# Value weights loaded as whole rows into both row halves, with a new order of the opening, in a linear attention and MLP kernel

## The chip, the cores and the metric

The kernel runs on one core of a Trainium2 chip. The metric is the device time of one execution in microseconds. The core has five engines with instruction queues of their own: TensorE (PE; its weight loads are shown as PEld), VectorE (DVE), ScalarE (ACT), GpSimd (POOL) and SyncE (SP), which here only issues DMAs. Each queue runs in order: an instruction that waits holds up all those behind it on its engine.

## What is computed

The input x has 2048 rows of 576 values in bfloat16. A pre-norm mixer with 32 heads of 18 dimensions is followed by a pre-norm MLP with 4608 hidden values:

```python
qkv = (x @ wqkv).reshape(B, S, 3, H, Dh)            # x: layer norm of the input
pq = jnp.einsum("bhsd,hdf->bhsf", q, w_phi)
pk = jnp.einsum("bhsd,hdf->bhsf", k, w_phi)
phi_q = concatenate([softmax(pq), softmax(-pq)])    # 36 features per head
phi_k = concatenate([softmax(pk), softmax(-pk)])
kv = jnp.einsum("bhsf,bhsd->bhfd", phi_k, v)
z = jnp.einsum("bhsf->bhf", phi_k)
num = jnp.einsum("bhqf,bhfd->bhqd", phi_q, kv)
den = jnp.einsum("bhqf,bhf->bhq", phi_q, z)[..., None] + 1e-6
h = x_in + (num / den) @ wo
out = h + gelu(layernorm(layernorm(h)) @ w1 + b1) @ w2 + b2
```

## The kernel before

The 2048 rows are 16 tiles of 128, taken in pairs p = 0 to 7; x stays in on-chip memory as `xh`. The contraction over 576 input features is done in nine chunks of 64 (`KC`, `KH`). One tile of a pair uses partitions 0 to 63 of TensorE and the other 64 to 127, side by side, so the weights `wkp` (keys), `wv` (values), `wqp` (queries) and `wo` have to stand in both halves of the partitions: rows `c * 64 + k` of the matrix at partition k, and again at 64 + k. This is `project` (L420): 9 chunks x 2 halves = 18 matmuls of 288 columns for one pair and half of the heads (`i` = 0 or 1).

The order of the whole kernel is written out by hand from L771 on, one call after the other, and the queues follow it. The opening does the following.

- **Loads.** `load_wk` (key weights), `load_x`, `load_values` (L163) and `load_wq` (L597, query weights, five DMAs in rows of 252 bytes) are all issued on SP. The value weights come in two DMAs, columns 0 to 287 and 288 to 575, each as 64 partitions x 9 chunks x 288 columns (rows of 576 bytes), to partitions 0 to 63 only.
- **Copies.** `copy_values` (L171) copies them on GpSimd into partitions 64 to 127, in four parts (column half i; chunks 0 to 4 or 5 to 8).
- **Key folds.** The key weights are turned (`flip_mm`, `flip_ev`) and multiplied per head with w_phi on TensorE: `fold_k_mm` (L376, ten matmuls for one chunk), and `fold_k_ev` (L388) moves the product from PSUM to `wkp`. The folds come in the order of chunks 0, 4, 8, 3, 7, 1, 2, 6, 5, and all nine are evacuated by ScalarE (the group L389).
- **Normalisation.** `stats` (L287, VectorE, two tiles per pair), `power` (L298, GpSimd, the inverse deviation), `centre` (L305, GpSimd) and `scale` (L308, ScalarE or VectorE) write the normalised pair to one of three buffers `lnb`. The pair is then turned, features onto partitions: pairs 0 and 1 on TensorE (`turn_x_mm`, `turn_x_ev`), the later ones by a DMA transpose on SP (`turn_dma`, L320).
- **Projections.** `key_mm` and `value_mm` project, `key_exp` (L458) writes exp(+) and exp(-) on ScalarE, `key_sum` (VectorE) and `key_weigh` (GpSimd) make the softmax of them, `value_ev` moves the values to `vals`, whose last column per head is 1 (`ones`, L224, GpSimd), and `sums` (L554) adds this tile's part to `acc_kv` in PSUM.

All the PSUM tiles of this stage but `acc_kv` come from the pool `two`, which has three buffers of two banks, taken in turn: a fold, a turned half pair or a projection can only start when the tile three before it has been evacuated. Per opening that is: folds 3 to 5, the two parts of `turn_x_mm(1)`, `key_mm(0, 0)`, `key_mm(0, 1)`, `value_mm(0, 0)` and so on.

SP's queue in the opening is, in order: key weights (three DMAs), x tiles 2 to 3 and 4 to 7, values (two), x tiles 8 to 11, query weights (five), `turn_dma(2)`, `load_wo(2)`, `turn_wq(4)`, `load_wo(0)`, `turn_wq(1)`, `turn_dma(3)`, the other `turn_wq`, `turn_dma(4)`, x tiles 12 to 15, `load_wo(3)`. A DMA on SP also waits until an earlier one, whose completion semaphore it takes over, has landed; there are eight of these for plain DMAs and transposes from SP and ScalarE together, used in turn.

Later on, `query_mm` and `query_exp` make the query features, `turn_q` transposes them on SP's queue, `combine_mm` multiplies them with the tables, and `divide` (L654, VectorE) divides by the denominators and writes `ob`, which is turned to `oT` and multiplied with `wo` (`residual_mm`, L692). The order of the features in `ob` has to be that of the rows of `wo`: before, place k = e * 32 + h of chunk c holds feature h * 18 + 2c + e, and `load_wo` (L606) fetches it in four DMAs (row half, e), each to 32 partitions in rows of 1152 bytes. From about 85 us on the MLP runs (`up`, `down`), with the other blocks' attention in between.

Of the kernel before, what the change touches and what calls it, by code (L numbers as in the profile page):

```python
# [8 lines left out]
P = 128  # L9
# [6 lines left out]
D = 576  # L16
NH = 32
DH = 18
# [7 lines left out]
HALF = D // 2  # L26
HH = NH // 2
VW = DH + 1
KC = 9
KH = 64  # L30
# [13 lines left out]
def kernel(  # L44
# [13 lines left out]
    nc = tc.nc  # L58
# [33 lines left out]
    wo = persist.tile([P, KC, D], BF16, name="wo", tag="wo")  # L92
# [10 lines left out]
    ob = [persist.tile([P, KC, 2, KH], BF16, name=f"ob{i}", tag=f"ob{i}") for i in range(2)]  # L103
# [56 lines left out]
            A_wqkv[0:512, D + f0 : D + f1].rearrange("(c p) f -> p c f", p=P),  # L160
        )

    def load_values(i):  # L163
        nc.sync.dma_start(
            wv[0:KH, :, i * HALF : (i + 1) * HALF],
            A_wqkv[:, 2 * D + i * HALF : 2 * D + (i + 1) * HALF].rearrange(
                "(c k) f -> k c f", k=KH
            ),
        )

    def copy_values(i, part, copy):  # L171
        cs = slice(i * HALF, (i + 1) * HALF)
        ks = slice(part * 5, 5 + part * 4)
        copy(wv[KH:P, ks, cs], wv[0:KH, ks, cs])  # L174

    wphi_rows = A_w_phi.rearrange("h d f -> (h d) f")

# [44 lines left out]
        )  # L222

    def ones():  # L224
        nc.gpsimd.memset(vals[:, :, :, DH], 1.0)

    def window_masks():
        full = small.tile([P, KW * WH], FP32, name="full", tag="full")
# [129 lines left out]
    def folded_whole(name, c, m):  # L358
        return flight[name, c].rearrange("p b f -> p (b f)")[:m, SPAN : SPAN + D]
# [13 lines left out]
    def turn_wq(c):  # L373
        nc.sync.dma_start_transpose(wT[:, :, c * P : (c + 1) * P], wq[:, c, :])

    def fold_k_mm(c):  # L376
        flight["k", c] = two.tile([P, 2, 512], FP32, name="pW", tag="two")[:, :, :]
        for g in range(NG):
            k = P if g < NG - 1 else 72
            for a in range(2):  # L380
                nc.tensor.matmul(
                    folded_part(g, "k", c, slice(a * KH, (a + 1) * KH)),
                    wT[:k, g, c * KH : (c + 1) * KH],
                    bd[:k, g, 0 : GH[g], :].rearrange("p h f -> p (h f)"),
                    start=True, stop=True,
                )

    def fold_k_ev(c, copy):  # L388
        copy(wkp[:, c, :], folded_whole("k", c, P))  # L389

    def fold_mm(name, c):
# [62 lines left out]
    phik, phiq, phiT = {}, {}, {}  # L454

    def key_mm(p, i):
        features("k", wkp, p, i, PLAIN)
# [139 lines left out]
    def load_wq():  # L597
        for c in range(NC):
            m = P if c < NC - 1 else 64
            src = A_wqkv[c * P : c * P + m, 0 : NG * 126]  # L600
            nc.sync.dma_start(
                wq[:m, c, :].rearrange("p (g f) -> p g f", g=NG)[:, :, 0:126],
                src.rearrange("p (g f) -> p g f", g=NG),
            )

    def load_wo(part):  # L606
        half, e = divmod(part, 2)
        r0 = half * KH + e * 32
        nc.sync.dma_start(
            wo[r0 : r0 + 32, :, :], A_wo.rearrange("(h c e) f -> e h c f", c=KC, e=2)[e]  # L610
        )

    def load_biases():
# [39 lines left out]
            leave_home(("phiT", p, a))  # L653

    def divide(t):
        o = ob[t // 2 % 2][:, :, t % 2, :].rearrange("p c (e h) -> p c e h", e=2)
        rec = small.tile([P, NH], FP32, name="rec", tag="rec")
        for w0, w1_ in BANKS:
            h0, h1 = FIRST[w0], min(NH, w1_ * WH)
            pv = products[t][w0 // 6][:, 0 : (h1 - h0) * VW].rearrange("p (h v) -> p h v", v=VW)  # L660
            nc.vector.reciprocal(rec[:, h0:h1], pv[:, :, DH])  # L661
            nc.vector.tensor_tensor(  # L662
                o[:, :, :, h0:h1],
                pv[:, :, 0:DH].rearrange("p h (c e) -> p c e h", e=2),
                rec[:, h0:h1].rearrange("p (u v h) -> p u v h", u=1, v=1).to_broadcast(
                    [P, KC, 2, h1 - h0]
                ),
                ALU.mult,
            )
# [107 lines left out]
    window_masks()  # L777
    load_x(2, 4)
    load_x(4, 8)
    load_values(0)  # L780
    load_values(1)
    stats(0, 1)
    power(0)
    centre(0, 0)
    scale(0, 0, act)
# [35 lines left out]
    fold_k_mm(7)  # L821
    fold_k_ev(7, act)
    fold_k_mm(1)
    fold_k_ev(1, act)
    fold_k_mm(2)
# [25 lines left out]
    load_wo(2)  # L851
    power(3)
    key_exp(0, 0)
    key_sum(0, 0)
    key_exp(0, 1)
    value_ev(0, 0, act)
    copy_values(1, 0, gps)
    turn_wq(4)
    load_wo(0)
    key_mm(1, 0)  # L860
# [70 lines left out]
    key_weigh(3, 1, 1, pool)  # L931
    fold_mm("q", 2)
    fold_ev("q", 2, act)
    load_wo(3)
    stats(6, 0)
    key_sum(3, 0)
    key_weigh(3, 1, 0, pool)
# [372 lines left out]
```

## Time and profile before

| what | us |
|---|---|
| median of 3 runs | 392.02 (391.94 to 392.32) |
| the profiled execution | 392.69 |
| its span | 391.0 |
| TensorE busy | 383.6 |
| VectorE, ScalarE, GpSimd busy | 163.5, 163.7, 128.2 |
| MLP matmuls, up (L1150) and down (L1194) | 141.3 and 143.3 |
| the four copies of the value weights (L174) | 5.0 |
| nine key fold evacuations on ScalarE (L389) | 5.06 |

The span runs from the first to the last instruction that the profiler saw; the execution's own time is 1.7 us longer. Times of single instructions count from the start of the span. Successive instructions of VectorE and ScalarE overlap by some 0.08 to 0.1 us in the records, so a row's duration is a little more than the pace at which such instructions follow each other. An entry of a timeline ends with the idle time before it and, after the arrow, what ended it.

### The profile page before, as it was taken

To read this page: it belongs to the slowest core of one execution; us is meant where nothing else is said; L and a number is where in the kernel's file an instruction comes from. 1 tells how busy PE (TensorE), PEld (TensorE's weight loads), DVE (VectorE), ACT (ScalarE), POOL (GpSimd) and SP (SyncE) were. 2 spreads that over 40 slices of the span, in tenths; PEclk is the share of its full clock that TensorE was granted. 3 is DMA by queue.
4 is the path that set the end of the run, shared out by engine and by line. 5 is a ranking of instruction groups with operands and counts; after the bars stand their busy time and mean duration, and the time that the engine had idled before them with its cause. 6 is when DMAs were issued, how large, how long until landed. Compare 5 with 4: busy or idle time off the path is not lost.

```text
span 391.0 us, 10251 instructions
## 1 busy us (share of the span) xinstructions
PE 383.6 (98%) x4492; PEld 267.2 (68%) x4493; DVE 163.5 (42%) x367; ACT 163.7 (42%) x290; POOL 128.2 (33%) x167
## 2 busy tenths in 40 slices
PE   8899999999999999999999999999999999999997
PEld 4687777779878887844457887444677764447773
DVE  6989894595249388590029322000480000000100
ACT  3978887678501850056650000666300026661000
POOL 8899999214604564144003111000031110000120
PEclk9999999999999999999999999999999999999999
DMA  8999749999655666643005542000041000000000
GB/s 220 189 182 175 163 98 184 227 300 254 206 106 104 95 107 134 107 61 62 0 2 63 90 106 48 16 1 2 2 102 50 17 17 0 2 2 0 17 29 18
DMA packets 76108, 34.76 MB, mean 89 GB/s; under 512 B 63026, under 2 KB 73536, under 8 KB 76064
## 3 DMA queue, kind: packets, MB, share of 16 engines
q1 hardware_dynamic: 75376, 32.47, 41.9%
q0 software_dynamic: 400, 1.35, 1.3%
q8 instruction: 35, 0.57, 0.6%
q10 hardware_dynamic: 288, 0.30, 0.3%
q14 instruction: 9, 0.07, 0.1%
HBM read 16.53 MB, written 2.36 MB: 48 GB/s over the span
## 4 chain that ended last, share of the span: by engine, by line
PE 94%; DVE 4%; POOL 1%; issue 1%; POOLq 0%
PE po L1194 36%; PE ph L1150 36%; PE pk L426 7%; PE pa L697 5%; PE pv L426 4%; PE acc_kv L562 2%; PE pw L250 1%; PE pn L648 1%; DVE st L293 1%; POOL wv L174 1%; DVE ob L662 0%; PE pW L396 0%; DVE shared L260 0%; PE pT L338 0%; DVE shared L314 0%
## 5 line engine op out<-in xcount | busy, mean ns | idle before, releaser
L1172 ACT ACTIVATE home<-ph,b1col 128x512 bf16<-128x512 f32 (+1 forms) x180 | 98.5, 598 | 169.6 <-PE ph L1150 166.3
L1194 PE MATMUL po<-w,home 128*128 128x288 bf16 (+2 forms) x1151 | 143.3, 286 | 0.1
L1150 PE MATMUL ph<-shared,w 64*128 64x512 bf16 (+2 forms) x1638 | 141.3, 332 | 0.1
L1194 PEld LDWEIGHTS <-home 128*128 128x128 bf16 x1152 | 109.2, 98 | 32.3 <-issue 1.8
L1150 PEld LDWEIGHTS <-w 64*128 64x128 bf16 x1638 | 80.3, 94 | 60.0 <-issue 1.0
L1198 DVE TENSOR_TENSOR ot<-po,hb 128x288 bf16<-128x288 f32 (+2 forms) x32 | 14.5, 454 | 106.5 <-PE po L1194 100.7
L1183 POOL TENSOR_TENSOR hb<-xh,b2bc 128x576 f32<-128x576 bf16 x16 | 20.4, 1272 | 104.6 <-DVE ot L1198 95.2
L426 PEld LDWEIGHTS <-home 64*128 64x128 bf16 x864 | 42.0, 94 | 10.8 <-issue 1.1
L512 POOL TENSOR_TENSOR padded<-home,rq 128x540 bf16<-128x540 bf16 x32 | 34.8, 1101 | 36.4 <-DVE rq L504 14.9
L256 POOL TENSOR_TENSOR rs<-va,mhalf 128x1 f32<-128x1 f32 x16 | 8.8, 550 | 105.0 <-DVE va L254 105.0
L706 DVE TENSOR_TENSOR xh<-pa,xh 128x288 bf16<-128x288 f32 x32 | 13.2, 449 | 71.6 <-PE pa L697 71.6
L483 POOL TENSOR_TENSOR phik<-phik,rk 128x576 bf16<-128x576 bf16 x32 | 36.4, 1164 | 1.4 <-PE pv L426 0.9
L477 DVE TENSOR_REDUCE sk<-phik 128x64 f32<-128x1152 bf16 x16 | 21.2, 1327 | 5.4 <-ACT phik L448 5.4
L448 ACT ACTIVATE home<-pk 128x576 bf16<-128x576 f32 x32 | 18.9, 649 | 6.9 <-PE pk L426 5.7
L503 DVE TENSOR_REDUCE sk<-home 128x64 f32<-128x1152 bf16 x16 | 21.0, 1313 | 0.0
L426 PE MATMUL pv<-wv,home 64*128 64x288 bf16 x288 | 20.9, 283 | 0.1
L426 PE MATMUL pk<-wqp,home 64*128 64x288 bf16 x288 | 20.0, 283 | 0.2 <-ACT home L448 0.2
L448 ACT ACTIVATE phik<-pk 128x576 bf16<-128x576 f32 x32 | 18.7, 652 | 3.1 <-PE pk L426 3.1
L426 PE MATMUL pk<-shared,home 64*128 64x288 bf16 x288 | 19.9, 283 | 0.0
L661 DVE RECIPROCAL rec<-pn 128x18 f32<-128x18 f32 (+1 forms) x32 | 8.0, 250 | 27.9 <-PE pn L648 27.9
L697 PE MATMUL pa<-wo,shared 64*128 64x288 bf16 x288 | 18.8, 283 | 0.0
L697 PEld LDWEIGHTS <-shared 64*128 64x128 bf16 x288 | 13.9, 94 | 4.3 <-issue 0.5
(78 smaller groups left out, 209.0 us busy)
## 6 DMA issues: line engine op xcount, KB each, us to landing
w<-in_B_w_dram SPq DMA_DIRECT2D x21, 432.0 KB, 7.0
out_dram<-ot SPq DMA_DIRECT2D x15, 144.0 KB, 1.9
xh<-in_A_x_dram SPq DMA_DIRECT2D x3, 576.0 KB, 7.3
wo<-in_A_wo_dram SPq DMA_DIRECT2D x4, 324.0 KB, 6.3
w<-in_B_w_dram POOLq DMA_DIRECT2D x3, 432.0 KB, 10.5
wv<-in_A_wqkv_dram SPq DMA_DIRECT2D x2, 324.0 KB, 9.9
w<-in_A_wqkv_dram SPq DMA_DIRECT2D x4, 157.5 KB, 8.7
wqp<-wqp SPq DMA_DIRECT2D x2, 288.0 KB, 3.9
```

Source lines behind the costliest of these rows:

```text
L426: nc.tensor.matmul(dst[:, a, 0:HALF], lhs[rows, c, :], w[rows, slot, i * HALF : (i + 1) * HALF], start=(n == 0), stop=(n == KC - 1),)
L448: nc.scalar.activation(rows[:, :, i * HH : (i + 1) * HH, s, :], flight[key, p, i][:, :, 0:HALF].rearrange("p a (h f) -> p a h f", f=DH), A ...
L477: nc.vector.tensor_reduce(sk[:, :, :], part_of(dst, i), AX.X, ALU.add)
L483: eng.tensor_tensor(part, part, flight["r" + key, p, i][:, a, :].rearrange("p (h o) -> p h o", o=1).to_broadcast([P, NH, DH]), ALU.mult,)
L503: nc.vector.tensor_reduce(sk[:, :, :], part_of(phiq[p], i), AX.X, ALU.add)
L512: eng.tensor_tensor(padded[:, a, g0 * P : (g0 + 5) * P].rearrange("p (g k) -> p g k", k=P)[:, :, 0:STEP].rearrange("p g (h f) -> p g h f", ...
L697: nc.tensor.matmul(pa[a], oT[p % 2][rows, c, :], wo[rows, c, cs], start=(c == 0), stop=(c == KC - 1),)
L1150: nc.tensor.matmul(ph[half][:, lo:hi], w1[p_ // 9][rows, c, p_ % 9 * P : (p_ % 9 + 1) * P], ln2T[rows, c, base + lo : base + hi], start=(c ...
L1172: nc.scalar.activation(hidden(m), ph[half][:, 0:width], AF.Gelu_apprx_tanh, bias=b1col[:, m : m + 1], scale=1.0,)
L1183: nc.gpsimd.tensor_tensor(hb[:, :], xh[:, t, :], b2bc[:, :], ALU.add)
L1194: nc.tensor.matmul(po[:, :], hidden(m)[:, i_ * P : (i_ + 1) * P], w2[m // 18][:, m % 18, cs], start=(j == 0), stop=(j == NM - 1),)
L1198: nc.vector.tensor_tensor(ot[:, cs], po[:, :], hb[:, cs], ALU.add)
```

## The change

The value weights come by DMA into both halves of the partitions, as whole rows of 576 columns (1152 bytes): `load_values(e, half, eng)` brings chunks 0 to 4 (e = 0) or 5 to 8 (e = 1) to the lower or the upper 64 partitions. There are four such DMAs, on SP's queue at the place of the two. The copies on GpSimd are gone.

```diff
-    def load_values(i):
-        nc.sync.dma_start(
-            wv[0:KH, :, i * HALF : (i + 1) * HALF],
...
-    def copy_values(i, part, copy):
-        cs = slice(i * HALF, (i + 1) * HALF)
-        ks = slice(part * 5, 5 + part * 4)
-        copy(wv[KH:P, ks, cs], wv[0:KH, ks, cs])
+    def load_values(e, half, eng):
+        c0, c1 = ((0, 5), (5, KC))[e]
+        eng.dma_start(
+            wv[half * KH : (half + 1) * KH, c0:c1, :],
+            A_wqkv[c0 * KH : c1 * KH, 2 * D : 3 * D].rearrange("(c k) f -> k c f", k=KH),
+        )
```

The opening is put in another order. `ones` goes to VectorE, ahead of the key flips. The fold of chunk 7 is evacuated by VectorE, both scalings of pair 1 follow right behind it on VectorE, and `stats(2, 1)`, `power(2)` and `stats(3, ...)` come later. `scale(2, 0)` moves to VectorE, and `scale(2, 1)` behind `key_exp(0, 0)` on ScalarE. `key_mm(0, 0)` takes the chunks in the order in which they were folded (`fold_order`).

```diff
     stats(2, 0)
-    ones()
     fold_k_mm(8)
     fold_k_ev(8, act)
     power(1)
-    stats(2, 1)
-    scale(1, 0, vec)
     fold_k_mm(3)
     fold_k_ev(3, act)
-    copy_values(0, 1, gps)
     fold_k_mm(7)
-    fold_k_ev(7, act)
+    fold_k_ev(7, dve)
+    scale(1, 0, vec)
+    scale(1, 1, vec)
...
     load_wq()
+    fold_k_ev(6, act)
+    turn_x_mm(1)
+    fold_k_ev(5, act)
+    stats(2, 1)
     power(2)
-    centre(2, 0)
-    stats(3, 0)
-    fold_k_ev(6, act)
-    scale(1, 1, vec)
-    stats(3, 1)
-    turn_x_mm(1)
     centre(2, 1)
-    copy_values(1, 1, gps)
-    copy_values(0, 0, gps)
     turn_x_ev(1, 0, dve)
-    fold_k_ev(5, act)
+    turn_x_ev(1, 1, dve)
     key_mm(0, 0)
     key_mm(0, 1)
+    key_exp(0, 0)
+    scale(2, 0, vec)
     scale(2, 1, act)
-    scale(2, 0, act)
     turn_dma(2)
-    turn_x_ev(1, 1, dve)
+    stats(3, 0)
+    stats(3, 1)
     stats(4, 0)
     stats(4, 1)
     value_mm(0, 0)
-    load_wo(2)
     power(3)
-    key_exp(0, 0)
```

`wo` comes in two DMAs, one for each half of the partitions, at the places of `load_wo(0)` and `load_wo(1)`; partition k holds rows 9k to 9k + 8 in one run. `divide` writes the features in the order that belongs to it: place k = 2h + e of chunk c holds feature h * 18 + 9e + c.

```diff
+    def load_wo(half):
         nc.sync.dma_start(
-            wo[r0 : r0 + 32, :, :], A_wo.rearrange("(h c e) f -> e h c f", c=KC, e=2)[e]
+            wo[half * KH : (half + 1) * KH, :, :],
+            A_wo.rearrange("(k c) f -> k c f", c=KC),
         )
...
             nc.vector.tensor_tensor(
-                o[:, :, :, h0:h1],
-                pv[:, :, 0:DH].rearrange("p h (c e) -> p c e h", e=2),
+                o[:, :, h0:h1, :],
+                pv[:, :, 0:DH].rearrange("p h (e c) -> p c h e", e=2),
```

The number of matmuls is the same, and no line from `key_mm(1, 0)` on moves, but for the places of the two pieces of `wo` that fall away.

More of the change, by code (lines that the diff above doesn't have):

```diff
@@ L224, in ones @@
     def ones():
-        nc.gpsimd.memset(vals[:, :, :, DH], 1.0)
+        nc.vector.memset(vals[:, :, :, DH], 1.0)
     def window_masks():
@@ L374, in turn_wq @@
         nc.sync.dma_start_transpose(wT[:, :, c * P : (c + 1) * P], wq[:, c, :])
+    fold_order = []
     def fold_k_mm(c):
@@ L388, in fold_k_ev @@
     def fold_k_ev(c, copy):
+        fold_order.append(c)
         copy(wkp[:, c, :], folded_whole("k", c, P))
@@ L456, in key_mm @@
     def key_mm(p, i):
-        features("k", wkp, p, i, PLAIN)
+        features("k", wkp, p, i, PLAIN if p or i else [(c, c) for c in fold_order])
     def key_exp(p, i):
@@ L604, in load_wq @@
             )
-    def load_wo(part):
-        half, e = divmod(part, 2)
-        r0 = half * KH + e * 32
+    def load_wo(half):
         nc.sync.dma_start(
-            wo[r0 : r0 + 32, :, :], A_wo.rearrange("(h c e) f -> e h c f", c=KC, e=2)[e]
+            wo[half * KH : (half + 1) * KH, :, :],
+            A_wo.rearrange("(k c) f -> k c f", c=KC),
         )
@@ L655, in divide @@
     def divide(t):
-        o = ob[t // 2 % 2][:, :, t % 2, :].rearrange("p c (e h) -> p c e h", e=2)
+        o = ob[t // 2 % 2][:, :, t % 2, :].rearrange("p c (h e) -> p c h e", e=2)
         rec = small.tile([P, NH], FP32, name="rec", tag="rec")
@@ L662, in divide @@
             nc.vector.tensor_tensor(
-                o[:, :, :, h0:h1],
-                pv[:, :, 0:DH].rearrange("p h (c e) -> p c e h", e=2),
-                rec[:, h0:h1].rearrange("p (u v h) -> p u v h", u=1, v=1).to_broadcast(
-                    [P, KC, 2, h1 - h0]
+                o[:, :, h0:h1, :],
+                pv[:, :, 0:DH].rearrange("p h (e c) -> p c h e", e=2),
+                rec[:, h0:h1].rearrange("p (u h v) -> p u h v", u=1, v=1).to_broadcast(
+                    [P, KC, h1 - h0, 2]
                 ),
@@ L779 @@
     load_x(4, 8)
-    load_values(0)
-    load_values(1)
+    load_values(0, 0, syn)
+    load_values(0, 1, syn)
+    load_values(1, 0, syn)
+    load_values(1, 1, syn)
     stats(0, 1)
+    ones()
     power(0)
@@ L856 @@
     value_ev(0, 0, act)
-    copy_values(1, 0, gps)
     turn_wq(4)
@@ L933 @@
     fold_ev("q", 2, act)
-    load_wo(3)
     stats(6, 0)
```

3 lines of the change are left out of this document (removed).

## The prediction

> **What bounds the kernel now.** I read first the page's busy shares and the chain that ended last.
>
> ```profile
> PE 383.6 (98%) x4492; PEld 267.2 (68%) x4493; DVE 163.5 (42%) x367; ACT 163.7 (42%) x290; POOL 128.2 (33%) x167
> ...
> PE 94%; DVE 4%; POOL 1%; issue 1%; POOLq 0%
> ```
>
> TensorE is busy for 98% of the span and carries 94% of the chain, at a granted clock of 1.00 in every window I read. From 20.8 us on the chain is almost wholly TensorE, so what counts is when TensorE gets past each place of the opening; what it loses there it does not win back. The timeline of TensorE (start, us, line; idle before it in brackets) shows where it loses:
>
> ```profile
> 11.42 2.63 PE L381 MATMUL pW<-w 128*64 128x126 bf16 x50 [0.15 <-ACT shared L389]
> 15.21 0.68 PE L338 MATMUL pT<-ident,shared 128*128 128x128 bf16 x9 [1.17 <-ACT shared L389]
> 15.82 2.38 PE L426 MATMUL pk<-shared,home 64*128 64x288 bf16 x36
> 18.04 1.50 PE L426 MATMUL pv<-wv,home 64*128 64x288 bf16 x18
> 19.27 1.36 PE L426 MATMUL pk<-shared,home 64*128 64x288 bf16 x18
> 20.38 2.77 PE L426 MATMUL pv<-wv,home 64*128 64x288 bf16 x36
> 22.88 2.47 PE L426 MATMUL pk<-shared,home 64*128 64x288 bf16 x36
> ```
>
> Between the last key fold and the turn of tile pair 1 (15.21) TensorE is idle for 1.17 us. After that a group of 18 matmuls takes 1.10 us, and the four groups from 18.04 to 22.88 take 4.84 instead of 4.40: 0.44 is lost on the value weights' copies, which the chain names too (its pieces in order of time: start, us, what):
>
> ```profile
> 16.84 1.38 POOL wv L174
> ...
> 19.35 1.39 POOL wv L174
> 20.78 2.36 PE pv L426 x35
> ```
>
> The last row that matters, 22.88, is `key_mm(2, 0)`. It reads tile pair 2, turned by `turn_dma(2)` on SP's queue. SP's timeline:
>
> ```profile
> 3.64 1.78 SPq L164 DMA_DIRECT2D wv<-in_A_wqkv_dram  x2
> 5.47 1.08 SPq L179 DMA_DIRECT2D xh<-in_A_x_dram  x1
> 6.59 10.97 SPq L601 DMA_DIRECT2D w<-in_A_wqkv_dram  x5
> 17.68 1.42 SPq L321 DMA_TRANSPOSE home<-shared  x1
> ```
>
> The five query weight issues keep SP for 10.97 us though an unhindered one (the first) takes 0.47: SP waits for queue space, which the transfers ahead, the values among them, free as they drain. Only then comes the transpose, which lands 4.1 us after its issue (list of DMA issues for that stretch): at 21.8, only 1.1 us before `key_mm(2, 0)`.
>
> **Gain of the new order.** The key folds run at 0.53 us each, the pace of ScalarE's evacuations (nine in 5.06 us), since each fold waits for one of three PSUM buffers. The change gives chunk 7 to VectorE. Its price: the nearest rows are 692 ns for 512 f32 values out of PSUM (L1198) and 443 ns for 576 bf16 values (L371); the first, with 64 more values, gives 0.76, and I take that. VectorE is free for it at 12.30, when the second statistics of the stretch are done (`stats(2, 1)` moves behind the scalings), so it ends at 13.05. Fold 6 waits for that buffer and runs 13.1 to 13.55, ScalarE empties it until 14.24, fold 5 runs until 14.05 and its evacuation ends at 14.77 instead of 15.17. The scalings `scale(1, 0)` and `scale(1, 1)` (0.43 apart) follow at 12.97 and end at 13.92 instead of 15.15, so the turn starts at 14.0 and ends by 14.6, and `key_mm(0, 0)` starts when the last fold's buffer is free: 14.8 instead of 15.82. **Gain 1.0.** Its bounds are 0.4 (what the evacuations alone give) and 1.17. The order of chunks in `fold_order` gives nothing, since the same buffer wait comes before it.
>
> The copies go with their 0.44, so TensorE would reach `key_mm(2, 0)` at 22.88 - 1.0 - 0.44 = 21.45. The gain of 1.43 is real if the data are there.
>
> **Price of the doubled value load.** Before, 2 x 324 KB go to 64 partitions in rows of 576 bytes; after, 4 DMAs bring 1,327,104 bytes, in rows of 1152, alternately to the lower and the upper 64. What such transfers run at is read from the windows (stretch and its length in us, granted clock, DMA share, GB/s):
>
> ```profile
> 7.00:8.00 1.00, 1.00 1.00 383
> 10.00:11.00 1.00, 1.00 1.19 180
> 44.00:45.00 1.00, 1.00 0.96 286
> 45.00:46.00 1.00, 1.00 1.02 204
> 46.00:47.00 1.00, 1.00 1.08 240
> 59.00:60.00 1.00, 1.00 1.06 205
> ```
>
> At 7 us a load to all 128 partitions moves 383 GB/s. At 10 the values of before, on 64, move 180: 663,552 bytes in 3.7 us. At 59 two w1 pieces for the same 64 partitions move 205. At 44 to 47 a w1 piece for the upper half follows one for the lower half, the nearest row to the new load: 286, 204 and 240, mean 243. So the new load takes 6.5 us at 204, 5.5 at 243, 3.5 at 383: 2.8 or 1.8 more than now, or 0.2 less. The burst at 286 is the start of a transfer and this one is long, so I take 225: 5.9 us, **2.2 more**.
>
> The Trainium skill, page "SBUF — State Buffer", section "Door 1: The DMA port swizzle", says that partitions 0 to 63 reach 8 of the 16 DMA ports and gives 196 GB/s for them against 328 for 128. The rows above agree (205 against 383); by its 196 the load would take 6.8 us, 3.1 more, and the time come out at 394.0.
>
> **The sum.** All that waits for queue space behind the values moves by 2.2: SP's last query weight issue, `turn_dma(2)` (its inputs are scaled by 17.9, no bound: `key_mm(0, 0)` ends at 15.9, two exponentials of 0.53 and a scaling of 0.87 follow on ScalarE) and its landing, 21.8 + 2.2 = 24.0. TensorE stands there from 21.45 and starts at 24.0, against 22.88 before: +1.1. So the rule is: loss = extra DMA time - 1.1. Behind that matmul on TensorE's queue stands everything else. The other new waits are covered: the last value piece lands at 15.2 + 2.2 = 17.4, and `value_mm(0, 0)` needs it at 17.65; x rows 8 to 11 land at 16.5 + 2.2 = 18.7, where VectorE now comes at 18.3 (0.4 lost there, and `sums(0, 0)` has 0.9 of room). `turn_dma(3)` waits for `scale(3, 1)`, which VectorE reaches 1.5 later than before (0.66 for the fold, 0.4 for `scale(2, 0)`, 0.4 waiting for `power(2)`): issued at 25.3 to 26, landed 3.9 later at 29.9 at worst, and needed at 30.12 + 1.1. This caps any gain: 25.3 + 3.9 = 29.2 is 0.9 before 30.12.
>
> Costed at nothing: the `ones` memset, 2.32 us on GpSimd, becomes 512 values on VectorE, by its memset of 320 values in 0.33 some 0.5 us, inside the 2.36 us that VectorE waits for TensorE before 7.57 (without that cover 0.5 is lost). GpSimd loses 5.0 us of copies; its weighing starts when VectorE's sums arrive, at 22.1 as now. wo in two pieces moves the same bytes to the same kind of half; two issues of about 0.6 fall away; the late piece (56.95, landing 7.8 later) doubles, 1.6 more at 205, ahead of `turn_q(0)`, which lands at 68.6 and is wanted at 71.1. The divide keeps 324 and 252 values per instruction (496 and 421 ns); only the walk changes, and the masked copy of the tables (L575, another walk) takes 498 for the same 324. So nothing; with no row for inner pairs the bound is double time on the four that the chain holds, +1.8, which I think remote. Nothing speaks for a gain there.
>
> The profiled execution took 392.69 us (span 391.0), so 393.8 by its own measure; it stands 0.67 above the median of 392.02, to which the same +1.1 is added: **393.1**.
>
> **The rivals.**
> - *The two halves overlap* (the other side, faster). If engines drift apart, some write the lower half while others write the upper, and the load runs at the 286 seen at 44 or better. At 276 GB/s (4.8 us) the loss is nil. From 330 (4.0 us, 0.35 more) the kernel is over 0.2% faster, and at 383 the gain is stopped by `turn_dma(3)` at 0.9: 391.1. For it: the burst at 44. Against it: 204 a microsecond later. Chance 0.18.
> - *Cover and cost cancel.* At 238 to 330 GB/s the extra is 0.35 to 1.9 us and the time within 0.78 us (0.2%) of now: about 392.2. Chance 0.22.
> - *No overlap at all.* The load runs at 204, as at 59, throughout: 2.8 more, +1.7, and 0.2 for x rows 8 to 11 that hold VectorE up by a further 0.6: 393.9. Chance 0.15. The Trainium skill, page "SBUF — State Buffer", section "Can I just issue two DMAs to hit both halves?", says that two such DMAs gain only 6% over one; the rows agree in part (243 against 205).
> - *The change doesn't do what it says*: the value pieces land too late for `value_mm(0, 0)` itself. From 2.45 us extra on that is so, but the wait lies inside the longer one at `key_mm(2, 0)` and adds nothing.
>
> **How the numbers follow.** Forecast (208 to 238 GB/s; 392.8 to 393.6) 0.45. With the third rival, slower by over 0.2% has 0.60; within it 0.22; faster 0.18. 0.2% (0.8 us) is about what a measurement of this kernel can tell from no change. The range takes in both ends of the load's price, 391.1 to 393.9, and 0.3 for the divides.
>
> **What would show it.** Right: `key_mm(0, 0)` near 14.8; no GpSimd copy of wv; DMA near 225 GB/s from 8 to 14; SP's query weight issues ending near 19.8; TensorE idle for 2 us and more before `key_mm(2, 0)` near 24, released by the transposed tile. Wrong: over 300 GB/s in that stretch, the transpose issued by 18.5, or divides far from 496 ns.

## The result and the profile after

The changed kernel takes 396.61 us (median of 5 executions, 395.12 to 397.2) against 392.13 (391.94 to 392.36) for the kernel before: 1.0103 times as long, 95% interval 1.0077 to 1.0128, so 4.5 us slower. The forecast had the side right and the size wrong: it said +1.1, and 396.61 is 2.4 above the upper end of its range. The profiled execution took 397.2, with a span of 395.5 (before 391.0). Helpers' lines have lower numbers after, since the copies are gone: `project` is L423, `turn_dma` L315, `load_wq` L598, `load_values` L165, `load_wo` L604, the fold's evacuation L386, the divide L658.

The page's busy shares and chain of the changed kernel:

```profile
PE 384.4 (97%) x4492; PEld 267.3 (68%) x4493; DVE 165.0 (42%) x370; ACT 162.5 (41%) x288; POOL 120.9 (31%) x161
...
PE 90%; ACT 3%; DMA 3%; DVE 2%; POOL 1%; issue 1%; POOLq 0%
```

TensorE has no more to do (384.4 against 383.6), but DMA, which had no share of the chain, now has 3%. The pieces of that chain, in order of time (start, us, what), name two transfers:

```profile
19.37 4.06 DMA home<-shared
23.48 1.29 PE pk L423 x18
...
25.99 7.12 DMA home<-shared
33.15 2.16 PE pk L423 x18
```

The same two places on TensorE's timeline (start, us; the idle time before in brackets):

```profile
14.44 2.38 PE L423 MATMUL pk<-shared,home 64*128 64x288 bf16 x36 [0.15 <-ACT shared L386]
16.64 1.28 PE L423 MATMUL pv<-wv,home 64*128 64x288 bf16 x18
17.75 1.28 PE L423 MATMUL pk<-shared,home 64*128 64x288 bf16 x18
18.85 2.38 PE L423 MATMUL pv<-wv,home 64*128 64x288 bf16 x36
23.48 2.38 PE L423 MATMUL pk<-shared,home 64*128 64x288 bf16 x36 [2.25 <-DMA home<-shared]
...
33.15 2.16 PE L423 MATMUL pk<-shared,home 64*128 64x288 bf16 x18 [2.37 <-DMA home<-shared]
35.10 2.10 PE L423 MATMUL pv<-wv,home 64*128 64x288 bf16 x18
37.04 1.14 PE L423 MATMUL pk<-shared,home 64*128 64x288 bf16 x16
```

The reader is to see three things. `key_mm(0, 0)` starts at 14.44 instead of 15.82. `key_mm(2, 0)` starts at 23.48 behind a wait of 2.25. And `key_mm(3, 0)`, at 30.12 before, starts at 33.15 behind a second wait of 2.37, after which groups of 18 matmuls that take 1.10 stand 1.95 apart. The windows (stretch, busy times, granted clock, DMA share, GB/s) say why:

```profile
10.00:11.00 1.00, 0.85 (x30) 0.73 (x26) 0.97 (x5) 1.00 (x3) 0.00 (x0) 1.00 1.08 233
12.00:13.00 1.00, 0.73 (x21) 0.61 (x22) 1.00 (x3) 1.00 (x3) 0.13 (x1) 1.00 1.10 226
...
33.00:34.00 1.00, 0.85 (x10) 0.61 (x12) 1.00 (x2) 0.00 (x0) 1.00 (x2) 0.69 1.28 277
34.00:35.00 1.00, 1.00 (x12) 0.66 (x10) 0.96 (x3) 0.00 (x0) 1.00 (x2) 0.50 1.28 277
35.00:36.00 1.00, 1.00 (x12) 0.63 (x10) 0.35 (x1) 0.65 (x2) 1.00 (x2) 0.50 1.04 148
36.00:37.00 1.00, 1.00 (x14) 0.65 (x10) 0.00 (x0) 0.54 (x2) 1.00 (x2) 0.60 0.82 276
```

Behind the second wait the granted clock is at 0.50 for 0.62 + 2.0 + 0.8 = 3.4 us (worked out from the means), half of which, 1.7 us, is lost. SP's timeline shows what stands ahead of the second transpose:

```profile
3.61 2.67 SPq L165 DMA_DIRECT2D wv<-in_A_wqkv_dram  x4
...
7.09 12.16 SPq L598 DMA_DIRECT2D w<-in_A_wqkv_dram  x5
19.37 2.41 SPq L315 DMA_TRANSPOSE home<-shared  x1
22.54 1.20 SPq L368 DMA_TRANSPOSE w<-w  x1
23.79 0.59 SPq L604 DMA_DIRECT2D wo<-in_A_wo_dram  x1
24.48 1.22 SPq L368 DMA_TRANSPOSE w<-w  x1
25.99 1.58 SPq L315 DMA_TRANSPOSE home<-shared  x1
```

Their times from issue to landing, from the list of DMA issues, are 4.1 for `turn_dma(2)`, 5.6 for wo, 6.3 for `turn_wq(1)` and 7.1 for `turn_dma(3)`: landings at 23.4, 29.4, 30.8 and 33.1, one behind the other.

From the two profiles the 4.5 us of span are: +0.6 at `key_mm(2, 0)` (+1.0 without the 0.42 by which the opening began sooner in this execution), +2.4 more at `key_mm(3, 0)` (33.15 - 30.12 = 3.03), and +1.7 from the clock: at the next key group, 37.04 against 32.32, it is +4.7, of which 0.2 is won back later.

### The profile page after: what moved, and what is told of

Its sections match the earlier page's. It is cut to its first block, busy times and chain, and to the rows that moved or that the text cites. A ratio compares the mean times of both kernels' runs of the same rounds, so it can differ in the third digit from the quotient of the medians.

```text
span 395.5 us, 10241 instructions
## 1 busy us (share of the span) xinstructions
PE 384.4 (97%) x4492; PEld 267.3 (68%) x4493; DVE 165.0 (42%) x370; ACT 162.5 (41%) x288; POOL 120.9 (31%) x161
## 4 chain that ended last, share of the span: by engine, by line
PE 90%; ACT 3%; DMA 3%; DVE 2%; POOL 1%; issue 1%; POOLq 0%
PE po L1185 36%; PE ph L1141 36%; PE pk L423 7%; PE pa L693 5%; PE pv L423 3%; DMA home<-shared 3%; PE acc_kv L559 1%; PE pn L644 1%; ACT shared L386 1%; ACT phik L445 1%; DVE ob L658 0%; PE pW L393 0%; ACT shared L266 0%; DVE shared L254 0%; PE pT L332 0%
## 5 line engine op out<-in xcount | busy, mean ns | idle before, releaser
L423 PEld LDWEIGHTS <-home 64*128 64x128 bf16 x864 | 42.4, 96 | 16.5 <-DMA home<-shared 5.5
L423 PE MATMUL pk<-shared,home 64*128 64x288 bf16 x288 | 20.6, 291 | 4.8 <-DMA home<-shared 4.6
L474 DVE TENSOR_REDUCE sk<-phik 128x64 f32<-128x1152 bf16 x16 | 21.2, 1323 | 8.0 <-ACT phik L445 7.9
L423 PE MATMUL pv<-wv,home 64*128 64x288 bf16 x288 | 21.0, 291 | 0.0
L423 PE MATMUL pk<-wqp,home 64*128 64x288 bf16 x288 | 19.8, 283 | 0.2 <-ACT home L445 0.2
L693 PE MATMUL pa<-wo,shared 64*128 64x288 bf16 x288 | 18.8, 283 | 0.0
```

The costliest lines, as they stand in the source:

```text
L423: nc.tensor.matmul(dst[:, a, 0:HALF], lhs[rows, c, :], w[rows, slot, i * HALF : (i + 1) * HALF], start=(n == 0), stop=(n == KC - 1),)
L474: nc.vector.tensor_reduce(sk[:, :, :], part_of(dst, i), AX.X, ALU.add)
L693: nc.tensor.matmul(pa[a], oT[p % 2][rows, c, :], wo[rows, c, cs], start=(c == 0), stop=(c == KC - 1),)
```

## The experiments

In each result the ratio is to the kernel before on the same chip. Two theories stood at the start. W: two separate causes, the values delaying `turn_dma(2)` and wo delaying `turn_dma(3)`, with the clock on top. V: the values' bytes alone delay both transposes.

### The three parts of the change, one at a time

The value load alone, in the kernel before (no copies, old order, wo in four pieces):

```diff
-    load_values(0)
-    load_values(1)
+    load_values(0, 0, syn)
+    load_values(0, 1, syn)
+    load_values(1, 0, syn)
+    load_values(1, 1, syn)
...
-    copy_values(0, 1, gps)
...
```

> The kernel before with one part of the change: the value weights by four DMAs of whole rows into both halves, no copies; order of the opening, wo and divide as before. Theory W: turn_dma(2) lands 1.7 us later than before, at 23.5, as in the changed kernel; key_mm(2, 0) starts 0.6 us later than the 22.9 of before; the wo pieces and turn_dma(3) follow SP's queue by about 1 us and have 2.4 us of room: time 392.4 to 393.2. Rival V: a second stall too, above 394.5.

Measured: 395.18, ratio 1.0068 (1.0044 to 1.0092), +2.9. Its timeline:

```profile
14.90 0.68 PE L332 MATMUL pT<-ident,shared 128*128 128x128 bf16 x9 [1.18 <-ACT shared L383]
15.51 2.38 PE L420 MATMUL pk<-shared,home 64*128 64x288 bf16 x36
...
25.05 2.38 PE L420 MATMUL pk<-shared,home 64*128 64x288 bf16 x36 [2.75 <-DMA home<-shared]
```

`turn_dma(2)` is issued at 18.66, only 0.98 later than before, but takes 6.3 instead of 4.1 to land. This part alone makes the kernel slower, and it does so through that one wait: there is none before `key_mm(3, 0)`. So the values do not delay both transposes by themselves. The wait is 1.5 us longer than theory W had it (landing at 25.0, not 23.5), and the time lies 2.0 above its range; in this profile a 16 KB packet of another queue was in flight from 21.38 to 23.41, of which the last part of the experiments tells.

wo in two pieces alone, with the divide's new walk, in the kernel before:

```diff
-    load_wo(2)
...
-    load_wo(3)
```

> The kernel before with nothing changed but wo in two pieces of 64 partitions (and the divide's views that go with it). Theory W (the whole first half of wo, 648 KB, stands ahead of turn_dma(3)): key_mm(3,0) waits 1 to 3 us, 393.3 to 395.5. Rival P (phase: what delays a transpose is that it falls together with an instruction fetch, and wo counts only by chance): turn_dma(3) lands as before, key_mm(3,0) starts at 30.1 to 30.4, 392.0 to 392.5.

Measured: 392.3, ratio 1.0006 (0.9995 to 1.0018). No wait before `key_mm(2, 0)` or `key_mm(3, 0)`; `turn_dma(3)` is issued at 23.55 and lands at 28.10, needed at 29.59. In the old order this part costs nothing that can be measured.

The new order alone, in the kernel before (value load, wo and divide as before; the four copies too, but at other places of GpSimd's queue):

```diff
...
+    copy_values(0, 0, gps)
+    copy_values(0, 1, gps)
     fold_k_mm(3)
     fold_k_ev(3, act)
-    copy_values(0, 1, gps)
     fold_k_mm(7)
-    fold_k_ev(7, act)
+    fold_k_ev(7, dve)
+    scale(1, 0, vec)
+    scale(1, 1, vec)
...
```

> The new order alone: value load, copies, wo's four pieces, their places and the divide as in the kernel before. With the value load alone at +3.0 and wo alone at 0.0 against the kernel before, and the whole change at +4.35, the order alone is +1.3 if the three add up. Theory Q (from 20 us on the transposes' queue, not TensorE's order, sets when the key projections start, so the 1.0 us gained at key_mm(0,0) is given back there): 392.2 to 393.7, key_mm(0,0) near 14.5 and a wait of 0.5 to 1.5 before key_mm(2,0) or key_mm(3,0). Rival (the step of the prediction: the order gains 1.0): 391.0 to 391.5, no such wait.

Measured: 393.11, ratio 1.0019 (1.0010 to 1.0028), +0.77. Its timeline:

```profile
14.80 2.38 PE L429 MATMUL pk<-shared,home 64*128 64x288 bf16 x36
...
22.47 2.38 PE L429 MATMUL pk<-shared,home 64*128 64x288 bf16 x36 [0.88 <-DMA home<-shared]
...
30.84 1.28 PE L429 MATMUL pk<-shared,home 64*128 64x288 bf16 x18 [1.06 <-DMA home<-shared]
```

The forecast's 14.8 for `key_mm(0, 0)` is there to the digit, and the gain of 1.0 is given back in two waits for transposes. `turn_dma(2)` is issued at 18.09, later than the 17.68 of before although TensorE is ahead, since `scale(2, 1)` now stands behind `key_exp(0, 0)`; `turn_dma(3)` is issued at 25.53 instead of 23.88. Theory Q is right. The three parts give 2.9 + 0.0 + 0.8 = 3.7 of the 4.5. The remaining 0.8 lies inside the intervals (those of the values alone and of the whole change are each some 2 us wide), so the medians do not show that the parts cost more together; that they meet at one place is read from the traces, in what follows.

### Where they meet: wo ahead of turn_dma(3)

The changed kernel with wo's first piece issued behind the x rows 12 to 15, after the transposes of this stretch:

```diff
-    load_wo(0)
     key_mm(1, 0)
...
     fold_ev("q", 2, act)
+    load_wo(0)
```

> The changed kernel with one edit: its first wo piece (648 KB) is issued behind x tiles 12 to 15, and no longer ahead of turn_wq(1) and turn_dma(3). Theory W (two causes: the value load delays turn_dma(2) by 0.6 us net, the doubled wo piece delays turn_dma(3), and the second stall halves TensorE's clock for 3.4 us): the stall before key_mm(2, 0) stays near 2.2 us, the one before key_mm(3, 0) is at most 0.3 us, the granted clock stays at 1.00, and the time is 392.3 to 393.0. Rival V (the values' bytes alone delay both transposes): key_mm(3, 0) still waits 2 us or more and the time stays above 395.

Measured: 394.9, ratio 1.0066 (1.0040 to 1.0091).

```profile
23.67 4.05 PE L423 MATMUL pk<-shared,home 64*128 64x288 bf16 x36 [2.22 <-DMA home<-shared]
...
32.49 1.27 PE L423 MATMUL pk<-shared,home 64*128 64x288 bf16 x18
```

`turn_dma(3)` is issued at 25.33, lands 3.3 later (28.6) and no wait is left before `key_mm(3, 0)` (32.49); the wait before `key_mm(2, 0)` (23.67, 2.22) stays, and in the profiled execution the halved clock now follows that one (36 matmuls take 4.05 instead of 2.38). So the second wait goes when wo goes, and the first does not. The waits are as theory W has them; the time is 1.9 above its range, which had no halved clock in it.

The changed kernel with wo in four pieces and the old divide:

```diff
...
     value_mm(0, 0)
+    load_wo(2)
     power(3)
...
```

> The changed kernel with wo in four pieces, and the divide's order, as before: 324 KB each, the first two on both sides of turn_wq(4), as in the kernel before. Theory W: the same bytes lie ahead of turn_dma(3) as in the changed kernel, only earlier in part, so the second stall shrinks but doesn't go: key_mm(3, 0) waits 0 to 1.5 us, time 392.5 to 395. If the size of one piece is what matters (a run of 10 KB per partition blocks the queues), the second stall is gone: 392.3 to 393.0. Rival V: no change, above 395.

Measured: 394.84, ratio 1.0066 (1.0043 to 1.0089). Waits of 2.22 at 23.49 and 0.89 at 31.68. The bytes of wo ahead of `turn_dma(3)` are the same 648 KB, but half of them leave right behind `turn_dma(2)`, as before, and not behind `turn_wq(4)`: its landing comes 1.5 sooner than in the changed kernel (31.6 against 33.1). Theory W had both the time and the second wait in its ranges.

The changed kernel with the old value load and its copies, wo in two pieces:

```diff
-    load_values(0, 0, syn)
...
+    load_values(0)
+    load_values(1)
```

> The changed kernel with the values loaded as before (two DMAs to the lower half) and copied by GpSimd, in the order column half 0, then 1. wo stays in two pieces. Theory W: turn_dma(2) is issued near 17.7 and key_mm(2, 0) waits at most 0.4 us; turn_dma(3), held by scale(3, 1) on VectorE and by the doubled wo piece, still lands late, 29.5 to 32, so key_mm(3, 0) starts 0 to 2 us later than the 30.1 of the kernel before: time 391.5 to 394.5. Rival V: both stalls go, 391.0 to 391.6.

Measured: 393.64, ratio 1.0031 (1.0017 to 1.0044).

```profile
22.99 2.38 PE L429 MATMUL pk<-shared,home 64*128 64x288 bf16 x36 [1.41 <-DMA home<-shared]
...
31.60 1.28 PE L429 MATMUL pk<-shared,home 64*128 64x288 bf16 x18 [1.31 <-DMA home<-shared]
```

Both waits remain, 1.41 at 22.99 and 1.31 at 31.60, though the doubled load is gone. Neither theory had room for a first wait without the doubled load: V falls, and W needs a third cause, the order itself. The run of the order alone, above, was made for that.

The order with the old value load and wo moved away (as in the first experiment of this section) should leave only the first wait's place:

```diff
-    load_values(0, 0, syn)
...
+    load_values(0)
+    load_values(1)
...
-    load_wo(0)
     key_mm(1, 0)
...
     fold_ev("q", 2, act)
+    load_wo(0)
```

> The changed kernel with the value load of before (one row half by DMA, copies on POOL) and with load_wo(0) issued behind load_x(12,16): what is left of the change is the new order of the opening and wo in two pieces off the path. Theory P (the order is good for 1.0 us, what eats it in the experiment with old values is the late turn_dma(2)): key_mm(0,0) near 14.5; without the large wo transfer turn_dma(3) lands under 4 us after its issue and no wait stands before key_mm(3,0); the wait before key_mm(2,0) is 1.4 as in the experiment with old values, if it comes from what happens before 23 us. 391.9 to 392.5. Rival (the order gains nothing by itself, it only moves the wait): 393 or more.

Measured: 393.69, ratio 1.0036 (1.0025 to 1.0046). `key_mm(0, 0)` at 14.84, waits of 1.01 at 22.65 and 0.46 at 30.41, and a new one of 1.09 at 43.25 for `turn_dma(5)`, which now stands behind wo. The rival is right. Moving a transfer away from one transpose put it ahead of another.

### Can the order's gain be kept?

Three versions, each shown against the one that it starts from. The version just above with `turn_dma(2)` brought forward:

```diff
-    copy_values(0, 1, gps)
...
     fold_k_ev(5, act)
+    copy_values(0, 1, act)
...
-    key_exp(0, 0)
     scale(2, 0, vec)
     scale(2, 1, act)
     turn_dma(2)
+    key_exp(0, 0)
```

> The order-only kernel with turn_dma(2) brought forward: key_exp(0,0) goes behind scale(2,1) on ACT, as in the kernel before, and copy_values(0,1) goes from POOL to ACT's idle time at 14.8 to 16.1, so that power(2) is not held up behind it. Theory P (the new order is good for 1.0 us if the transposes of rows 8 to 11 are over before the 16 KB fetch at about 20): turn_dma(2) issued near 17.1 instead of 18.1, landed by 21.0, key_mm(2,0) at 21.4 to 21.7 without a wait, 390.9 to 391.7, the first version under the kernel before. Rival (the transposes fall behind whatever goes before them, or TensorE then waits for ACT's later key_exp(0,0) or the later copies): key_mm(2,0) not before 22.3, 392 to 393.7.

Measured: 393.35, ratio 1.0033 (1.0020 to 1.0046). `turn_dma(2)` is issued at 16.93 as meant, 1.2 sooner, and lands at 22.4, 0.2 sooner: 5.5 us in flight. The theory fails on the landing; the rival is right.

The same with work put ahead of the wait, and wo behind `turn_dma(5)`:

```diff
+    value_mm(1, 0)
+    value_ev(1, 0, act)
     key_mm(2, 0)
     key_mm(2, 1)
     stats(5, 0)
-    value_mm(1, 0)
...
     turn_dma(5)
+    load_wo(0)
```

> The kernel with turn_dma(2) brought forward (new order, old value load), in which value_mm(1,0) and its eviction run ahead of key_mm(2,0), so that TensorE has 1.1 us of work while turn_dma(2) lands, and load_wo(0) is issued behind turn_dma(5) instead of ahead of it, where a wait of 1.06 before a later key_mm had come up. Theory R (the order's 1.0 us is real and was lost in these two waits, 0.97 and 1.06): both gone, 393.35 - 2.0 = 391.3, between 391.0 and 391.8, under the kernel before. Rival (transposes land later still, or another wait takes their place): 392.0 to 393.4.

Measured: 393.77 (392.94 to 395.51), ratio 1.0045 (1.0028 to 1.0062). The profiled execution (393.11) has lost the wait before `key_mm(2, 0)`, and has waits of 0.54 at 29.73, for `turn_dma(3)`, and 0.69 at 46.71, for the turned query weights. In place of each wait taken away the next transfer in line is waited for. Theory R fails, and the median is above the rival's range too.

The same two edits in the changed kernel, with its doubled value load:

> The changed kernel with its own value load and with the same two edits (value_mm(1,0) ahead of key_mm(2,0), load_wo(0) behind turn_dma(5)). Theory R plus C (what the change loses are waits for transposes, and half the clock behind a wait over 2 us): the wait before key_mm(2,0) falls from 2.2 to 1.1 and the clock is not halved, no wait before key_mm(3,0): 392.6 to 393.3. Rival (the doubled value load costs TensorE time elsewhere too): 394 or more.

Measured: 393.92 (392.58 to 394.82), ratio 1.0043 (1.0026 to 1.0060). Waits of 0.25, 0.44 and 0.49 in the profiled execution (393.03). The time lies between the two ranges: theory R plus C had no wait before `key_mm(3, 0)`. With its wait covered, the doubled load costs no more than the old one (393.92 against 393.77), so most of its price is the wait. No version with the new order came out under the kernel before.

### The clock

The changed kernel with ten matmuls of 512 columns ahead of `key_mm(3, 0)`, in its own bank and overwritten by it, so that TensorE works while it waits:

```diff
+        if (key, p, i) == ("k", 3, 0):
...
+            for _ in range(10):
+                nc.tensor.matmul(pk[:, 0, :]..., ident[:, :], wide, start=True, stop=True)
```

> The changed kernel with ten matmuls of 512 columns (10 x 0.213 us at full clock) ahead of key_mm(3,0), written to its own bank and overwritten by it, so that TensorE is not idle while it waits for turn_dma(3). Theory C (the idle of 2.4 us brings the clock to 0.5 for 3.4 us, which is 1.7 us of the loss): no stretch at 0.5 behind 33 us, key_mm(3,0) still near 33.1, the time 1.2 to 1.8 below the changed kernel's 396.6 (394.8 to 395.4), with less spread between its runs. Rival (the halved clock is a trait of that one execution and no part of the median): the time within 0.4 of 396.6.

Measured: 396.45 (396.16 to 396.9), ratio 1.0105 (1.0092 to 1.0118). No execution has a mean clock under 0.999, but the median falls by only 0.16: the theory's 1.2 to 1.8 is not there. In the profiled execution the waits themselves were longer (`key_mm(2, 0)` at 24.11, `key_mm(3, 0)` at 33.79), and from there to the next fold it takes 5.04 instead of 6.71, which is the 1.7. The query group that starts at 79.53 in the kernel before starts at 82.92 here and at 84.06 in the changed kernel, so up to there the filling has gained 1.1; but between there and 116 us this execution loses 0.8 (116.11 against 111.90 before, +4.2) that the changed kernel's profile does not (116.43, +4.5 at both places). So the gain exists in one trace and is not shown in the median.

The version with wo late has one wait, so there the question is cleaner; nine such matmuls ahead of `key_mm(2, 0)`:

```diff
+        if (key, p, i) == ("k", 2, 0):
...
+            for _ in range(9):
+                nc.tensor.matmul(pk[:, 0, :]..., ident[:, :], wide, start=True, stop=True)
```

> The changed kernel with load_wo(0) late (one wait is left, 2.2 us before key_mm(2,0), and in three of four executions a mean clock of 0.995 to 0.996) plus nine matmuls of 512 columns into key_mm(2,0)'s own bank ahead of it, so that TensorE does not stand idle there. Theory C (a wait of 2.2 us costs 1.7 more when the clock is halved behind it): mean clock 0.999 to 1.0 in every execution, key_mm(2,0) still near 23.6, 393.2 to 393.9 with all runs near the one undisturbed value of 393.5. Rival (the clock counts for nothing in the median): 394.6 to 395.1 as without the filling.

Measured: 393.94 (393.73 to 394.32), ratio 1.0045 (1.0031 to 1.0059).

```profile
24.41 2.38 PE L423 MATMUL pk<-shared,home 64*128 64x288 bf16 x36 [0.81 <-DMA home<-shared]
```

The mean clock was 0.999 or 1.0 in all five; without the filling the time was 394.9, and three of four executions had 0.995 or 0.996. The median is 1.0 less, just over the theory's upper end and below the rival's range, though `turn_dma(2)` landed at 24.4 in its profile, 0.7 later. The 36 matmuls behind the wait take 2.38 here and 4.05 without the filling: in that trace the halved clock is a part of the loss. For the medians it is likely and not shown, since the intervals of the two ratios overlap (1.0040 to 1.0091 and 1.0031 to 1.0059).

The changed kernel once more, unaltered:

> The changed kernel once more, for the spread between its executions. Theory P plus C (the two waits depend on where the instruction fetches and the transposes meet, and on the clock): the wait before key_mm(2,0) again 2.0 to 2.6, key_mm(3,0) between 32 and 34, the time 395 to 397.2. Rival (the second wait was a trait of that one execution): no wait over 1 us before key_mm(3,0).

Measured, in one execution: 396.21, waits of 1.66 at 22.83 and 2.81 at 32.95, clock 1.00 throughout. Both waits come back in other sizes and with no halved clock; so this execution is not slow for the clock. At the first MLP matmul it is 2.6 behind the kernel before (87.81 against 85.26), and from there to 115 us it loses 1.0 more (115.43 against 111.90), idle times of 0.36 and 0.22 in the MLP among it, which the changed kernel's first profile does not.

What the halved clock costs the changed kernel's median stays open. The executions with a mean clock of 0.995 or 0.996 took 395.24, 396.61 and 397.2, those with 1.0 took 395.12, 396.72 and, here, 396.21. Of 75 executions of the kernel before five had 0.995 or 0.996, with a median of 393.17 against 392.23 for the others.

### What holds a transpose up in flight

In the traces the transposes' packets (256 bytes each) all but stop now and then. The order-alone kernel shows it; windows of 0.4 us (last column GB/s) and the queue line for 19.4 to 20.8 (packets, MB, share):

```profile
19.40:19.80 0.40, 0.40 (x10) 0.37 (x8) 0.40 (x3) 0.40 (x2) 0.40 (x1) 1.00 1.25 283
19.80:20.20 0.40, 0.40 (x11) 0.37 (x8) 0.40 (x2) 0.40 (x2) 0.30 (x2) 1.00 4.96 76
20.20:20.60 0.40, 0.40 (x12) 0.38 (x8) 0.37 (x3) 0.40 (x2) 0.28 (x2) 1.00 0.00 0
20.60:21.00 0.40, 0.40 (x11) 0.37 (x8) 0.40 (x1) 0.40 (x2) 0.32 (x2) 1.00 0.06 13
...
21.40:21.80 0.40, 0.19 (x4) 0.00 (x0) 0.37 (x2) 0.40 (x1) 0.10 (x1) 1.00 1.28 291
```

```profile
q8 instruction: 1, 0.02, 5.7%
```

One packet of 16 KB of the queue that the profile calls instruction is in flight there, from 19.45 to 20.71, and around its end hardly a transpose packet starts. Counted over all traces of this study, for the 21 such packets at 17 to 36 us that met a transpose at work (over 550 of its packets started in the us before): per us, 786 packets start in the us before, 452 while it lasts (0.99 us in the median), 158 in the us behind it, 639 in the next (medians). Two runs move these packets. 39 more TensorE instructions at the start, in the same time, bring them 1.1 to 4.0 us forward:

```diff
-        for _ in range(n):
-            nc.tensor.matmul(pw[:, :, :], ident[:, :], wide, start=True, stop=True)
+        for j in range(4 * n):
+            nc.tensor.matmul(pw[:, j % 4, :], ident[:, :], ident[:, :], start=True, stop=True)
```

In the new order with the old value load and wo late:

> The order-only kernel with the thirteen warm-up matmuls of 512 columns made fifty-two of 128 columns: the same columns and time, 39 more TensorE instructions ahead of everything, so that the 16 KB instruction fetches fall some 2 us earlier against the transposes. Theory P (a DMA transpose stands still while a fetch is under way): turn_dma(2)'s landing moves by 1 us or more against the order-only kernel, toward earlier if the fetch at 19.4 moves out of it (then no wait before key_mm(2,0), 390.8 to 391.5). Rival B (the transposes are late for the bytes queued ahead of them): key_mm(2,0) within 0.3 of the order-only kernel, time within 0.4.

Measured: 394.52 (393.18 to 395.15), ratio 1.0056 (1.0044 to 1.0068). In its profile, the fastest of its executions, that packet comes at 18.17 instead of 20.07 in the version that it starts from, `turn_dma(2)` is issued at 17.80 and lands 3.4 later, at 21.2, where it took 4.5, and `key_mm(2, 0)` starts at 21.42 without a wait, 1.5 sooner than in the kernel before. But 1.1 us are lost again between 103 and 112 us, where TensorE waits three times for MLP weights (0.6 in all), and the median is higher, not lower. The landing moved as the theory says; the time did not follow.

In the kernel before:

> The kernel before with its thirteen warm-up matmuls of 512 columns made fifty-two of 128 columns (same columns and time, 39 more TensorE instructions), nothing else. Theory P (where the 16 KB instruction fetches fall against the transposes decides when these land): the fetches at 15.8, 21.0 and 28.0 come some 2 us earlier and the landings of turn_dma(2) and turn_dma(3) move by over 0.5; the time moves by over 0.3, more likely up, since these two have only 1.1 and 2.4 of slack, or the spread of its runs grows. Rival (the fetches do not matter): landings within 0.4, time within 0.2 of the kernel before, same spread.

Measured: 392.22, ratio 0.9999 (0.9990 to 1.0008). The packets come at 14.3, 18.1 and 26.9 instead of 15.8, 21.0 and 28.0. `turn_dma(2)` takes 5.2 instead of 4.1 and `turn_dma(3)` 5.4 instead of 3.9, yet no wait for a transpose arises: `key_mm(2, 0)` starts at 22.62, `key_mm(3, 0)` at 29.86. The flights grew by 1.2 and 1.6 us and the landings moved by 0.6 and 1.3, as the theory says; the kernel before has the slack for it (1.1 and 2.4), so the rival is right on the time.

The flights of `turn_dma(3)` in the 17 profiles sort by two things, what stands ahead of it and whether such a packet starts while it is in flight (one that starts within 0.1 us of its landing not counted):

| us in flight | no wo ahead | two pieces of 324 KB | one of 648 KB |
|---|---|---|---|
| no packet | 2.8 to 3.3 (3 profiles) | 3.9, 4.2 | 4.5 (1 profile) |
| a packet | 4.5 to 4.7 (4) | 5.3 to 5.8 (3) | 6.0 to 7.3 (4) |

In all eleven with a packet it lands 0.8 to 1.2 us after the packet's end. So wo ahead and the packet each lengthen the flight. The changed kernel's 7.1 has both, and the trace of before, with 3.9, was spared the packet by 0.2 us (landing at 27.73, packet from 27.95). A longer flight is also likelier to meet a packet, so the sorting alone does not prove the second cause. What holds these transposes up is not settled in full: the packets of the instruction queue meet many of the stops, but the transpose of 16.93 to 22.4 also stood still from 18.8 to 19.6 with no such packet in flight.

## Why the prediction came out as it did

- **Gain of the new order, 1.0 at `key_mm(0, 0)`.** Right: 14.80 in the order-alone run. VectorE's fold evacuation took 0.705 (0.76 forecast). As a part of the time it is worth nothing: alone, that order costs 0.77.
- **Price of the doubled value load.** The rate was right (233, 219 and 226 GB/s from 10 to 13 us; 225 forecast), and in the first profile so was the landing: `turn_dma(2)` at 23.4, `key_mm(2, 0)` at 23.48 behind 2.25 of idle time, 24.0 and 2.55 forecast, in an execution that began 0.42 sooner. SP's last query weight issue ended at 19.25 (19.8 forecast). In part this is luck: over the eight profiles with this load `turn_dma(2)` is issued 1.0 to 2.1 us later than in the kernel before and lands between 22.8 and 25.0, so 2.2 is just above the upper end. What the forecast had too short is the old load, 3.7 us by its bytes at 180 GB/s: the x tiles ahead of it land at 10.45 and its second piece at 15.18, which is 4.7. The Trainium skill, page "SBUF — State Buffer", section "Can I just issue two DMAs to hit both halves?", puts the gain of two such DMAs at 6%; here the kernel before moves 180, 199 and 192 GB/s from 10 to 13 us, so the gain is some 19%, with the bytes of all queues counted: more than the Trainium skill's 6%, and far from double.
- **"The other new waits are covered", `turn_dma(3)` "issued at 25.3 to 26, landed 3.9 later at 29.9 at worst".** This is the step that failed. The issue, 25.99, was inside the bounds; the flight was 7.1 and not 3.9, and 33.1 is past the 31.2 at which it was needed. The 3.9 was the same transpose's flight in the trace of before, taken as if it were a property of the transfer. It depends first on what stands ahead of it in the queue: `turn_dma(2)` landing 1.7 later than before, then `turn_wq(4)`, then wo; with wo moved away it was 3.3. It depends also on the 16 KB packets of the instruction queue, one of which was in flight here from 31.11 to 32.08: where wo was moved away and one was met, the flight was 4.5 to 4.7, and with the queue of before it was 5.4 when only these packets were moved. The Trainium skill, page "DMA: Bandwidth & Descriptors", section "Queues, rings and completion order", says that each DMA engine consumes descriptors in the order of its ring; the landings at 23.4, 29.4, 30.8 and 33.1 agree.
- **"wo in two pieces moves the same bytes", costed at nothing.** Right in the old order (+0.04), wrong in the new one. The forecast counted the bytes and not their place: the half that left at 19.15 behind `turn_dma(2)` now leaves at 23.79, right ahead of `turn_dma(3)`. By the profile with four pieces this is 1.5 of the 3.0 at `key_mm(3, 0)`.
- **No term for the clock.** The forecast read it as 1.00 and let TensorE stand for 2.5 us without asking what a wait of that size does. It cost 1.7 us in the profiled execution; its part in the median is open. The Trainium skill, page "TensorE: Matmul & The Clock Gate", section "Why this matters for your kernels", warns of idle gaps over about 3 us; here one of 2.37 was followed by the half clock and one of 2.81 was not, so the traces have a lower and less certain limit.
- **The sum.** In the profiled execution 0.6 was lost at the first wait (+1.1 forecast), 2.4 more at the second and 1.7 by the clock (nothing forecast for either), and 0.2 was won back: 4.5. That these are also the 4.5 of the medians is in part chance, since other executions of the changed kernel take as long with the clock at 1.00 throughout.
- **The divides** take 496 and 420 ns at most and least, as before (496 and 421), and `ones` on VectorE 0.485 in idle time: costed rightly at nothing.
- **The rivals.** None ended where the time did; the overlap of the two halves at 286 GB/s and more was not seen (204 to 266 from 8 to 15 us).

## What to carry to other kernels

A DMA's time from issue to landing is not a constant to be added to a new issue time: list what stands ahead of it in the queue, in order, and ask where each moved transfer now leaves. When the engine that bounds the kernel gets past a place sooner, look for the next transfer that it will wait for; here an order that gains a microsecond of TensorE time ahead of a chain of transfers that stays where it is gained nothing. And price a new wait of two microseconds or more on TensorE with the clock that may follow it.

## What the runs showed of the hardware

- Idle times of TensorE of 2.37 (changed kernel) and 2.22 us (wo late) were followed by a granted clock of 0.50 for 3.4 us; others of 2.22 (wo in four pieces), 2.25, 2.37 (the first wait of the version with ten matmuls), 2.75 and 2.81 were not. So the length alone does not decide it. Nine executions had matmuls in a wait, and their mean clock was 0.999 to 1.0.
- DMA transposes of 288 KB tiles took 2.8 to 8.0 us from issue to landing (83 of them in 17 profiles), and a 16 KB packet of the instruction queue goes with a loss of some 1.2 to 1.4 us of a transpose's progress (an estimate from the next four numbers), most of it in the microsecond behind the packet (786, 452, 158, 639 packets per us). Why it does so, no run here shows.
- Of 75 executions of the kernel before 59 lie within 0.4 us of their median, and the whole spread is 1.9; versions with waits for transposes spread over 0.5 to 2.6. But wo alone, with no such wait in its profile, spreads over 2.4 too, so the spread cannot be put down to these waits alone.
